# Column tiles of 64 for the attention read and the state product of an mLSTM plus mixture-of-experts kernel

## The chip, the cores and the metric

The kernel runs on one core of a Trainium2 chip. The metric is device time of one launch in microseconds; the median of three runs of the kernel before is 427.37 us (427.31 to 427.56).

## What is computed

A gated recurrent attention (2 batches, 8 heads, 768 steps, head size 40) is followed by four dense experts (320 to 1024 to 320), whose outputs are summed with normalised weights:

```python
for t in range(S):
    m_new = np.maximum(f_gate[:, :, t] + m, i_gate[:, :, t])
    f_stab = np.exp(f_gate[:, :, t] + m - m_new)
    i_stab = np.exp(i_gate[:, :, t] - m_new)
    m = m_new
    C = f_stab[:, :, None, None] * C + i_stab[:, :, None, None] * np.einsum('bhd,bhe->bhde', vt, kt)
    n = f_stab[:, :, None] * n + i_stab[:, :, None] * kt
    h_tilde = np.einsum('bhde,bhe->bhd', C, qt)
    denom = np.maximum(np.abs(np.einsum('bhd,bhd->bh', n, qt)), 1.0)[:, :, None]
    y[:, :, t] = h_tilde / ((1.0 + np.exp(-o_gate[:, :, t])) * denom)
...
for e in range(E):
    out += p[:, e:e + 1] * (np.maximum(x @ w1[e], 0.0) @ w2[e])
```

## The kernel before, in words

The 1536 tokens are 12 chunks `n` of 128; chunks 0 to 5 are the first batch, 6 to 11 the second, and `c = n % 6` is the place in the batch. Within a chunk the recurrence is written as matrix products. In the order in which TensorE (PE) gets them in the loop from chunk 2 on:

- `inter(n)` (L460, tile y1): queries times the state carried into the chunk, two heads to a product; left out at c = 0. ScalarE (ACT) then reads y1 out of PSUM head by head with a scale, eight instructions at L467 (tile yb).
- `intra(n)` (L474, tile y0): the chunk's own keys. One product for each of the 8 heads: the weighted scores `pm` of a head (128 keys x 128 queries) are loaded as weights, and the head's scaled values (64 columns, 41 of them used: 40 values and the sum) are streamed.
- `state(n)` (L427, tile st): what the chunk adds to the state, two heads to a product: 104 columns of keys as weights, 105 columns of values streamed. Of each product only the two diagonal blocks are wanted. Left out at c = 5. VectorE (DVE, L442) adds them to the decayed old state, at c = 0 ACT copies them (L76).
- `scores(n + 1)` (L412, tile s): keys times queries of the next chunk, two heads in two row tiles of 64 rows, side by side.

These are float32 products; each one stands in the trace as two weight loads (LDWEIGHTS, row PEld) and two MATMUL passes. Around them PE runs pieces of expert 0 on finished chunks (`steps`: hidden layer at L147, tile ph; output layer at L178 to L180, tile po) and the transposes of a finished chunk (`turn`, L500, tile px: two blocks of 128 columns and one of 64). `norm(n)` on DVE (L486 to L493) adds yb to y0, divides, and applies the output gate; `decay` (L385), `weigh` (L418) and `turn_lo` (L507, L508) are also on DVE. `values` and `keys` (L396, L401) and most of the splits of the experts' weights into a high and a low part (L92) are on GpSimd (POOL).

The order on every engine is the order of the code: chunks 0 and 1 are written out by hand (L556 to L617), the loop at L624 does chunks 2 to 11, and from about 165 us on only experts 1 to 3 are left. Nothing reorders a queue. The PSUM tiles y1, y0, st and px come in this order from the pool `ps_y`, which has two buffers (tag `y`): st(n) takes the buffer of y1(n), so its first product waits until ACT has read y1; px takes that of y0; y0 of the next chunk that of px. In chunks 0 and 1 some of these tiles come from other pools, by the arguments of the calls.

Of the kernel before, what the change touches and what calls it, by code (L numbers as in the profile page):

```python
# [15 lines left out]
B, H, S, D = 2, 8, 768, 40  # L16
NE, DM, FF = 4, 320, 1024
NT = B * S
L = 128
# [24 lines left out]
def tile_mlstm_moe(ctx, tc, gt, qk, vk, ot, dp, w1, w2, out):  # L44
    ctx.enter_context(tc.manual_schedule())
    nc = tc.nc
# [27 lines left out]
    def copy(eng, dst, src):  # L74
        if eng is nc.scalar:
            eng.activation(dst, src, AF.Copy)  # L76
        else:
            eng.tensor_copy(dst, src)
# [114 lines left out]
    with ExitStack() as actx:  # L193
# [166 lines left out]
        fbs, dds, vvs, pms, ss = {}, {}, {}, {}, {}  # L360
# [59 lines left out]
        def state(n, pool=ps_y, tag="y"):  # L420

            c, vv, kk = n % NC, vvs[n], kp[n % 2]
            if c == NC - 1:
                return
            st = pool.tile([L, NP, L], F32, tag=tag, name="st")
            for p in range(NP):
                nc.tensor.matmul(  # L427
                    st[0:104, p, 0:105],
                    kk[:, 2 * p:2 * p + 2, :].rearrange("k r d -> k (r d)")[:, 0:104],
                    vv[:, 2 * p:2 * p + 2, :].rearrange("k r d -> k (r d)")[:, 0:105],  # L430
                    start=True, stop=True,
                )
            cout = cs[(c + 1) % 2]
            if c == 0:
                for r in range(2):
                    q, q2 = slice(64 * r, 64 + 40 * r), slice(64 * r, 64 + 41 * r)
                    copy(nc.scalar, cout[q, :, q2], st[q, :, q2])
            else:
                cd = cds.pop(n)
                for q in (slice(0, 64), slice(64, 104)):  # L440
                    q2 = slice(q.start, q.start + (64 if q.start == 0 else D + 1))
                    nc.vector.tensor_add(cout[q, :, q2], cd[q, :, q2], st[q, :, q2])  # L442

        def carry(n):
# [26 lines left out]
        def intra(n):  # L471
            y = y0s[n] = ps_y.tile([L, H, 64], F32, tag="y", name="y0")
            for h in range(H):
                nc.tensor.matmul(  # L474
                    y[:, h, :], pms[n][:, h, :], vvs[n][:, h, :], start=True, stop=True
                )

        def norm(n):

# [90 lines left out]
        gate_i(2, NC, nc.gpsimd)  # L570
        decay(1)
        intra(0)
        state(0, ps_w, "w")
        values(1)
        keys(1)
# [11 lines left out]
        quarter_lo(0)  # L587
        gate_b(2, NC)
        intra(1)
        norm(1)  # L590
        turn(0, ps_h, "ph")
# [4 lines left out]
        turn_lo(1)  # L596
        scores(2)
        state(1)
        quarter_hi(1)
        gate_last(2, NC)  # L600
# [23 lines left out]
        for n in range(2, NCH):  # L624
            j, cc = n // 2, n % 2
            k = SLOTS[n - 2]
# [18 lines left out]
            if n == 3:  # L645
                weights_out(4, nc.gpsimd)
            intra(n)
            state(n)
            norm(n)
            if n == 2:  # L650
# [131 lines left out]
```

## Time and profile before

| | |
|---|---|
| median of three runs | 427.37 us |
| profiled execution, first to last instruction (span) | 425.8 us |
| PE busy with matmuls | 420.6 us |
| chunks (attention and expert 0) | up to about 165 us |
| experts 1 to 3 | from about 165 us |

The profile page gives the span of the profiled execution and no other time of it; the median stands 1.5 us above that span, which is what lies around it. Busy time of PE is the union of its passes, whose ends are modelled. A row of the chain of waits gives the time by which a piece of work carries the end further; a row of the timeline gives when a merged group starts and how long it takes from its first start to its last end, and in brackets how long the engine sat idle before it and for whom.

### The profile page before, as it was taken

What the parts mean: (1) busy time and instruction counts of PE and PEld (TensorE: products, weight loads), DVE (VectorE), ACT (ScalarE), POOL (GpSimd) and SP (SyncE); (2) the same over time, 40 slices, a digit from 0 to 9 for tenths busy, and PEclk for the clock granted to TensorE, in tenths of its full rate; (3) what the DMA queues carried; (4) which work ended last, traced back from release to release, by engine and by line L of the source; (5) the groups of instructions that cost most, each with busy time, mean ns of one, the idle gap of its engine ahead of it and who ended that gap; (6) DMA issues with size and microseconds to landing.
All of it is one profiled execution on the core that took longest, in us unless ns stands there. A gap on an engine that the chain in (4) does not pass through costs nothing.

```text
span 425.8 us, 6596 instructions
## 1 busy us (share of the span) xinstructions
PE 420.6 (99%) x2754; PEld 377.8 (89%) x2754; DVE 180.0 (42%) x321; ACT 125.3 (29%) x298; POOL 81.0 (19%) x92
## 2 busy tenths in 40 slices
PE   9999999999999999999999999999999999999996
PEld 5789999999999998897997988979979879789796
DVE  8869777574865321513313224123132242231321
ACT  5656233234313252503403124024031140120210
POOL 6855601220210170200610001007100010000000
PEclk9999999999999999999999999999999999999999
DMA  7984716347200002210110003001200000001001
GB/s 220 315 257 127 212 52 160 113 101 237 84 2 2 0 16 110 77 72 0 66 58 0 2 0 149 0 3 33 92 0 2 0 0 32 31 2 46 18 15 48
DMA packets 15078, 29.31 MB, mean 69 GB/s; under 512 B 1000, under 2 KB 10728, under 8 KB 13736
## 3 DMA queue, kind: packets, MB, share of 16 engines
q1 hardware_dynamic: 15048, 28.88, 21.5%
q8 instruction: 22, 0.36, 0.4%
q14 instruction: 8, 0.07, 0.1%
HBM read 26.86 MB, written 2.02 MB: 68 GB/s over the span
## 4 chain that ended last, share of the span: by engine, by line
PE 98%; DVE 1%; ACT 0%; issue 0%; DVEq 0%
PE ph L147 39%; PE po L178 13%; PE po L179 13%; PE po L180 13%; PE y L474 5%; PE s L412 3%; PE ph L170 3%; PE st L427 2%; PE y L460 2%; PE pwm L69 2%; PE px L500 1%; PE fb L368 1%; PE pit L298 0%; ACT cs L76 0%; PE pit L320 0%
## 5 line engine op out<-in xcount | busy, mean ns | idle before, releaser
L147 PE MATMUL ph<-xst,w1s 128*128 128x512 f32 (+1 forms) x888 | 171.0, 349 | 0.0
L147 PEld LDWEIGHTS ph<-xst,w1s 128*128 128x128 f32 x888 | 140.2, 189 | 27.7 <-issue 6.6
L178 PE MATMUL po<-w2s,h 128*128 128x320 f32 x384 | 119.5, 311 | 0.0
L156 ACT ACTIVATE h<-ph 128x512 fp32r<-128x512 f32 x96 | 57.4, 598 | 209.7 <-PE ph L147 209.0
L180 PE MATMUL po<-w2s,h 128*128 128x320 f32 x384 | 118.6, 309 | 0.0
L179 PE MATMUL po<-w2s,h 128*128 128x320 f32 x384 | 118.6, 309 | 0.0
L157 DVE SCALAR_TENSOR_TENSOR h<-ph,h 128x512 fp32r<-128x512 f32 x96 | 66.2, 690 | 116.0 <-ACT h L156 115.6
L178 PEld LDWEIGHTS po<-w2s,h 128*128 128x128 f32 x384 | 72.1, 188 | 0.9
L179 PEld LDWEIGHTS po<-w2s,h 128*128 128x128 f32 x384 | 72.1, 188 | 0.4
L180 PEld LDWEIGHTS po<-w2s,h 128*128 128x128 f32 x384 | 72.1, 188 | 0.0
L185 DVE SCALAR_TENSOR_TENSOR acc<-po,pw,acc 128x320 f32<-128x320 f32 x36 | 19.8, 550 | 100.0 <-PE po L180 100.0
L92 POOL TENSOR_TENSOR w1s<-raw,w1s 128x512 fp32r<-128x512 f32 (+1 forms) x24 | 23.6, 1020 | 58.2 <-ACT w1s L89 58.2
L385 DVE TENSOR_TENSOR_SCAN dd<-fb,id 128x512 f32<-128x512 f32 x24 | 29.3, 1264 | 0.2
L92 POOL TENSOR_TENSOR w2s<-raw,w2s 128x640 fp32r<-128x640 f32 x6 | 9.4, 1571 | 103.9 <-ACT w2s L89 103.9
L474 PE MATMUL y<-vp,pm 128*128 128x64 f32 x192 | 23.1, 273 | 0.7 <-DVE xst L508 0.7
L474 PEld LDWEIGHTS y<-vp,pm 128*128 128x128 f32 x192 | 22.5, 192 | 1.0 <-issue 0.8
L183 ACT ACTIVATE acc<-po,pw 128x320 f32<-128x320 f32 x12 | 6.3, 528 | 45.2 <-PE po L180 45.2
L467 ACT ACTIVATE yb<-y,ibT 128x41 f32<-128x41 f32 x80 | 16.0, 311 | 3.9 <-PE y L460 3.9
L418 DVE TENSOR_TENSOR pm<-s,dd 128x512 f32<-128x512 f32 x24 | 15.4, 682 | 0.5 <-PE s L412 0.3
L401 POOL TENSOR_TENSOR kp<-vk,dd 128x320 f32<-128x320 f32 x10 | 7.4, 735 | 38.4 <-DVE dd L385 38.4
L412 PE MATMUL s<-qk 64*128 64x128 f32 (+1 forms) x192 | 14.1, 285 | 0.0
L412 PEld LDWEIGHTS s<-qk 64*128 64x128 f32 (+1 forms) x192 | 11.8, 187 | 1.8 <-DVE pm L418 0.8
(94 smaller groups left out, 259.3 us busy)
## 6 DMA issues: line engine op xcount, KB each, us to landing
raw<-in_w SPq DMA_DIRECT2D x3, 1536.0 KB, 6.2
fb<-f_d SPq DMA_DIRECT2D x8, 512.0 KB, 7.6
raw<-in_w SPq DMA_DIRECT2D x3, 1280.0 KB
qk<-in_qk SPq DMA_DIRECT2D x4, 832.0 KB
vk<-in_vk SPq DMA_DIRECT2D x4, 640.0 KB, 8.1
acc<-in_ot SPq DMA_DIRECT2D x6, 320.0 KB, 9.2
out<-acc SPq DMA_DIRECT2D x12, 160.0 KB, 1.8
qk<-in_qk SPq DMA_DIRECT2D x4, 416.0 KB
```

Of the source, the lines that this page charges most:

```text
L92: eng.tensor_sub(lo, raw, hi.bitcast(F32))
L147: nc.tensor.matmul(ph[:, i, :], self.w1s[:, wi, f * L:(f + 1) * L], xst[:, xi, self.t0:self.t0 + n], start=(k == 0 and not self.e), stop=( ...
L156: nc.scalar.activation(hh, ph, AF.Relu)
L157: nc.vector.scalar_tensor_tensor(out=hl, in0=ph, scalar=0.0, in1=hh.bitcast(F32), op0=ALU.max, op1=ALU.subtract)
L178: nc.tensor.matmul(po, hh[:, sl], ws[:, LO, f, :], start=(f == 0), stop=False)
L179: nc.tensor.matmul(po, hh[:, sl], ws[:, HI, f, :], start=False, stop=False)
L180: nc.tensor.matmul(po, hl[:, sl], ws[:, HI, f, :], start=False, stop=(f == NF - 1))
L185: nc.vector.scalar_tensor_tensor(out=acc[:, i, :], in0=po, scalar=pw[:, i, e:e + 1], in1=acc[:, i, :], op0=ALU.mult, op1=ALU.add,)
L385: nc.vector.tensor_tensor_scan(out=dds[n][:, 4 * i:4 * i + 4].rearrange("p h t -> p (h t)"), data0=fbs[n][i].rearrange("p h t -> p (h t)") ...
L412: nc.tensor.matmul(ss[n][r][:, p, :], kg[q, p], qg[q, p], start=True, stop=True)
L467: nc.scalar.activation(yb[:, h], y1[:, h, 0:D + 1], AF.Copy, scale=ibT[:, c, i:i + 1])
L474: nc.tensor.matmul(y[:, h, :], pms[n][:, h, :], vvs[n][:, h, :], start=True, stop=True)
```

## The change

`intra` issues two products for each head instead of one: queries 0 to 63 and queries 64 to 127 as weights of 64 columns each, with results in PSUM partitions 0 to 63 and 64 to 127 of the same bank. The values streamed are the 41 used columns, no longer 64. `state` issues one product for each head instead of one for each pair: 40 columns of keys as weights, 41 columns of values streamed; the even head's result goes to partitions 0 to 39, the odd head's to 64 to 103. In both, two neighbouring products use the two column tiles of TensorE (128 rows x 64 columns). The additions at L442 and the copies at L76 take the two diagonal blocks of 40 x 41 instead of 64 x 64 and 40 x 41. Nothing else is changed.

```diff
             st = pool.tile([L, NP, L], F32, tag=tag, name="st")
+            blocks = [(slice(64 * r, 64 * r + D), slice(64 * r, 64 * r + D + 1)) for r in range(2)]
             for p in range(NP):
-                nc.tensor.matmul(
-                    st[0:104, p, 0:105],
-                    kk[:, 2 * p:2 * p + 2, :].rearrange("k r d -> k (r d)")[:, 0:104],
-                    vv[:, 2 * p:2 * p + 2, :].rearrange("k r d -> k (r d)")[:, 0:105],
-                    start=True, stop=True,
-                )
+                for r, (q, q2) in enumerate(blocks):
+                    h = 2 * p + r
+                    nc.tensor.matmul(
+                        st[q, p, q2], kk[:, h, 0:D], vv[:, h, 0:D + 1], start=True, stop=True
+                    )
...
-                for q in (slice(0, 64), slice(64, 104)):
-                    q2 = slice(q.start, q.start + (64 if q.start == 0 else D + 1))
+                for q, q2 in blocks:
                     nc.vector.tensor_add(cout[q, :, q2], cd[q, :, q2], st[q, :, q2])
...
             for h in range(H):
-                nc.tensor.matmul(
-                    y[:, h, :], pms[n][:, h, :], vvs[n][:, h, :], start=True, stop=True
-                )
+                for t in (slice(0, 64), slice(64, L)):
+                    nc.tensor.matmul(
+                        y[t, h, 0:D + 1], pms[n][:, h, t], vvs[n][:, h, 0:D + 1],
+                        start=True, stop=True,
+                    )
```

On PE, chunk 3 before, with what each instruction waits for (a name like Activation_49 is the semaphore of that engine; rows without brackets follow their predecessor): read of the old state, read of the own keys, state product, next scores, output layer.

```order
L460 MATMUL y_591<-cs_129,qk_131 128x128 x4
L474 MATMUL y_609<-vp_125,pm 128x64 [waits PE_49,DVE_49,Activation_49,Pool_49]
L474 MATMUL y_609<-vp_125,pm 128x64 x7
L427 MATMUL st<-vp_125,kp_127 104x105 [waits PE_49,Activation_49,Pool_49]
L427 MATMUL st<-vp_125,kp_127 104x105 x3
L412 MATMUL s<-qk_130 128x128 [waits DMAHW3_49]
L412 MATMUL s<-qk_130 128x128 x7
L178 MATMUL po<-w2s_93,h 128x320 [waits DVE_49]
```

The same place on PE in the changed kernel:

```order
L458 MATMUL y_627<-cs_129,qk_131 128x128 x4
L473 MATMUL y_645<-vp_125,pm 64x41 [waits PE_49,DVE_49,Activation_49,Pool_49]
L473 MATMUL y_645<-vp_125,pm 64x41 x15
L430 MATMUL st<-vp_125,kp_127 40x41 [waits PE_49,Activation_49,Pool_49]
L430 MATMUL st<-vp_125,kp_127 40x41 x7
L412 MATMUL s<-qk_130 128x128 [waits DMAHW3_49]
L412 MATMUL s<-qk_130 128x128 x7
L178 MATMUL po<-w2s_93,h 128x320 [waits DVE_49]
```

No instruction has moved past another: 8 products have become 16 and 4 have become 8, of smaller shape, and the first state product still waits for the same three engines. On DVE, the state addition of chunk 1 (cs, from the old state cd and st), with its neighbours:

```order
 L508 TENSOR_TENSOR xst<-px,xst 64x128
-L442 TENSOR_TENSOR cs_128<-cd,st 64x4x64
-L442 TENSOR_TENSOR cs_128<-cd,st 40x4x41
+L440 TENSOR_TENSOR cs_128<-cd,st 40x4x41 x2
 L385 SCALAR_TENSOR_TENSOR dd<-fb,id_117 128x512 x2
 L157 SCALAR_TENSOR_TENSOR h<-ph,h 128x512 x2
```

It is two instructions as before, the first of them smaller, in the same place.

## Rows read from the trace of the kernel before

**Rows 1.** The page: busy time of the engines; the chain that ended last, by line.

```profile
PE 420.6 (99%) x2754; PEld 377.8 (89%) x2754; DVE 180.0 (42%) x321; ACT 125.3 (29%) x298; POOL 81.0 (19%) x92
...
PE ph L147 39%; PE po L178 13%; PE po L179 13%; PE po L180 13%; PE y L474 5%; PE s L412 3%; PE ph L170 3%; PE st L427 2%; PE y L460 2%; PE pwm L69 2%; PE px L500 1%; PE fb L368 1%; PE pit L298 0%; ACT cs L76 0%; PE pit L320 0%
```

**Rows 2.** Instructions writing y and st: ns minimum/median/maximum, first and last start.

```profile
L474 PEld LDWEIGHTS y<-vp,pm x192: 186/192/192, 12.9 to 141.4; 128*128 128x128 f32 x192
L474 PE MATMUL y<-vp,pm x192: 217/275/323, 12.9 to 141.5; 128*128 128x64 f32 x192
L460 PE MATMUL y<-cs,qk x80: 272/275/377, 16.5 to 139.7; 104*128 104x128 f32 x80
...
L427 PEld LDWEIGHTS st<-vp,kp x80: 166/172/172, 14.7 to 131.4; 128*104 128x104 f32 x80
L427 PEldq EVENT_SEMAPHORE  x8: 51/1636/1641, 32.0 to 129.1; - x8
```

**Rows 3.** Chain of waits, chunks 4 to 6: start us, us, what.

```profile
63.62 0.33 PE px L500 x3
63.95 1.91 PE ph L147 x16
...
66.75 1.73 PE y L474 x16
68.49 1.09 PE s L412 x16
...
80.80 0.77 PE st L427 x8
...
82.66 4.03 PE ph L147 x32
```

**Rows 4.** Timeline, chunk 7: start us, us, engine, line, instructions, idle before.

```profile
89.65 1.90 PE L474 MATMUL y<-vp,pm 128*128 128x64 f32 x16
...
89.85 1.60 ACT L467 ACTIVATE yb<-y,ibT 128x41 f32<-128x41 f32 x8 [0.30 <-PE y L460]
...
91.55 0.95 PE L427 MATMUL st<-vp,kp 128*104 128x105 f32 x8
```

**Rows 5.** Timeline, chunks 0 and 1: ACT and DVE.

```profile
14.35 0.63 ACT L272 ACTIVATE ib<-ib 16x512 f32<-16x512 f32 x1 [1.11 <-POOL ib L271]
...
15.75 0.70 ACT L76 ACTIVATE cs<-st 64x256 f32<-64x256 f32 x2 [0.77 <-PE st L427]
...
17.01 1.30 DVE L277 TENSOR_TENSOR_SCAN gat<-fs,bs 16x512 f32<-16x512 f32 x1
...
17.69 1.60 ACT L467 ACTIVATE yb<-y,ibT 128x41 f32<-128x41 f32 x8 [1.01 <-PE y L460]
...
19.49 0.51 DVE L486 TENSOR_TENSOR y<-y,yb 128x328 f32<-128x328 f32 x1 [1.18 <-PE y L474]
```

**Rows 6.** Timeline, chunks 2 to 4.

```profile
31.77 2.33 DVE L385 TENSOR_TENSOR_SCAN dd<-fb,id 128x512 f32<-128x512 f32 x2
...
34.56 0.76 DVE L442 TENSOR_TENSOR cs<-cd,st 64x256 f32<-64x256 f32 x2 [0.47 <-PE st L427]
...
36.95 0.49 DVE L493 TENSOR_TENSOR xr<-xr,y 128x320 f32<-128x320 f32 x1
...
37.58 0.52 PE L500 MATMUL px<-ident,xr 128*128 128x128 f32 x3
...
43.24 3.98 POOL L92 TENSOR_TENSOR w2s<-w2r,w2s 128x640 fp32r<-128x640 f32 x2 [4.99 <-ACT w2s L89]
...
47.36 0.33 PE L178 MATMUL po<-w2s,h 128*128 128x320 f32 x1
...
53.46 1.55 ACT L467 ACTIVATE yb<-y,ibT 128x41 f32<-128x41 f32 x8
...
53.84 1.97 PE L474 MATMUL y<-vp,pm 128*128 128x64 f32 x16 [0.67 <-DVE xst L508]
...
55.65 0.93 PE L427 MATMUL st<-vp,kp 128*104 128x105 f32 x8
```

More of the change, by code (lines that the diff above doesn't have):

```diff
@@ L425, in state @@
             st = pool.tile([L, NP, L], F32, tag=tag, name="st")
+            blocks = [(slice(64 * r, 64 * r + D), slice(64 * r, 64 * r + D + 1)) for r in range(2)]
             for p in range(NP):
-                nc.tensor.matmul(
-                    st[0:104, p, 0:105],
-                    kk[:, 2 * p:2 * p + 2, :].rearrange("k r d -> k (r d)")[:, 0:104],
-                    vv[:, 2 * p:2 * p + 2, :].rearrange("k r d -> k (r d)")[:, 0:105],
-                    start=True, stop=True,
-                )
+                for r, (q, q2) in enumerate(blocks):
[3 more added lines that the diff above has]
+                    )
             cout = cs[(c + 1) % 2]
             if c == 0:
-                for r in range(2):
-                    q, q2 = slice(64 * r, 64 + 40 * r), slice(64 * r, 64 + 41 * r)
+                for q, q2 in blocks:
                     copy(nc.scalar, cout[q, :, q2], st[q, :, q2])
@@ L439, in state @@
                 cd = cds.pop(n)
-                for q in (slice(0, 64), slice(64, 104)):
-                    q2 = slice(q.start, q.start + (64 if q.start == 0 else D + 1))
+                for q, q2 in blocks:
                     nc.vector.tensor_add(cout[q, :, q2], cd[q, :, q2], st[q, :, q2])
```

## The prediction, made before the changed kernel ran

> **What bounds the kernel now.** I read the page first: PE is busy 420.6 of 425.8 us, and the chain that ended last is PE nearly throughout [rows 1]. The work that is changed is in that chain: the read of the own keys (L474) with 5% and the state product (L427) with 2%, some 30 us together. So time taken from these passes is time taken from the kernel, unless PE then has to wait for something. Three questions follow: what sets the pace of these passes, what a change of tiles costs, and who is late next in each chunk.
>
> **The pace of a pass.** I went to the durations of the single instructions [rows 2] and the chain around chunks 4 to 6 [rows 3]. A chunk's 16 passes of L474 take 1.73 us, 108 ns each; the 8 of L427 take 0.77 us, 96 ns each. Is it the load or the stream? A load of 128 columns is recorded with 192 ns, one of 104 columns with 172: 20 ns for 24 columns, 0.83 ns a column. A stream of 64 columns that isn't held up is recorded with 217 ns (the minimum of L474), one of 128 columns with 272 (L460): 55 ns for 64 columns, 0.86 ns a column. At L474 128 columns are loaded (107 ns) and 64 streamed (55 ns) while a pass takes 108, and the median MATMUL has 275 ns, 58 above its minimum: it is held up by its load. So the load sets the pace, one pass for each load, and what is streamed hides behind it.
>
> By this, a pass with 64 columns to load takes 108 - 64 x 0.83 = 55 ns, with 41 columns streamed (35 ns) behind it. A pass of the state product with 40 columns to load takes 96 - 64 x 0.83 = 43 ns.
>
> **Two tiles side by side.** The trace has no column tiles in this form, but it has row tiles: the scores (L412) run 16 passes of 128 columns in 1.09 us in two tiles of 64 rows [rows 3]. Taking 0.19 us off for the change of tiles (below), this is 0.90 us for 8 pairs, 112 ns a pair: two tiles together take as long as one pass of one tile. This is the nearest row, and I take the same for column tiles. Then the 32 passes of the new L474 are 16 pairs of 55 ns, 0.88 us, and the 16 of the new state product are 8 pairs of 43 ns, 0.34 us. Taken away: **0.85 us** a chunk from the first, **0.43 us** from the second. The other end is that two column tiles take turns: 32 x 55 = 1.76 and 16 x 43 = 0.69 us, which is +0.03 and -0.08 us: no gain. That end is the first rival.
>
> **Changing tiles.** After the scores, 32 passes of L147 take 4.03 us, though 16 take 1.91 where nothing is changed ahead of them [rows 3]: 4.03 - 2 x 1.92 = 0.19 us for leaving the row tiles, and the same for entering them. The other bound is the transposes: the third block of L500 has 64 columns, and three blocks take 0.33 us, with 16 passes of L147 in 1.91 behind them [rows 3]: nothing. The changed kernel has 15 more such places: into L473 ahead of ten chunks from 2 on, out of it after chunk 11, two around it in chunk 1, and one behind each state product of chunks 0 and 1. I take 0.19 for each, since the scores are the nearer relation (ordinary products in tiles of half size); zero stays in the range.
>
> The Trainium skill, "TensorEngine Tiling (Array Packing)", section "Key Properties", states that a change of the tiling mode drains TensorE. The row of the scores agrees with it, the row of the transposes shows no drain; by the rule each of the 15 places costs as taken here, by the second row none, and the sum below would be 0.95 us larger.
>
> **Who is late next.** The first state product takes the PSUM buffer of y1 and waits for ACT to have read it. In chunk 7 ACT reads from 89.85 for 1.60 us, to 91.45; the state product starts at 91.55 [rows 4], and the wait of PE's sequencer for this is 1.64 us long in the median of 8 [rows 2]. PE loses nothing by it today only because L474 fills just this time. When L474 is shorter, PE sits idle until 91.55 all the same: in chunks 3 and 7 to 10, which look alike, **the whole gain of L474 becomes a wait**, and the drain ahead of it is hidden there too. The scores, the output layer and all behind them wait in the same queue. Only what the state product saves remains.
>
> The sum, chunk by chunk:
>
> - Chunks 0 and 1. State product 0 ends 1.28 us earlier, but ACT is busy until 14.98, so its copy starts at 14.98 instead of 15.75 [rows 5]: 0.77 us. The read of y1 in chunk 1 then ends at 19.29 - 0.77 = 18.52; DVE's scan ends at 18.31; so norm(1), today at 19.49 and waiting for L474 [rows 5], starts at about 18.62. That is 0.87 us, and the transposes that wait for it move with it. State product 1 adds 0.43, less 0.19 for leaving column tiles: **1.11**.
> - Chunk 2. PE could gain 0.5, but the transposes at 37.58 follow DVE's xr (end 37.44), and DVE can add the state no earlier than its scan ends, at 34.10 instead of 34.56 [rows 6]: **0.46**.
> - Chunk 3. The output layer at 47.36 comes just behind POOL's split of w2, which ends at 47.22 [rows 6] and hangs on ACT, which starts it behind the read of y1. This chain isn't shortened: **0**. The 0.43 us of the state product are waited away.
> - Chunk 4. L474 waits for DVE at its start (0.67 us idle, which hides the drain). ACT's read ends at 55.01, so the state product can start at 55.11 instead of 55.65 [rows 6]: 0.54 + 0.43 = **0.97**.
> - Chunk 5 has no state product: 0.85 - 0.19 = **0.66**.
> - Chunk 6 has no y1: 0.85 + 0.43 - 0.19 = **1.09**.
> - Chunks 7 to 10: 4 x 0.43 = **1.72**.
> - Chunk 11: 0.85, less two drains, 0.38: **0.47**.
>
> Together 6.48 us: a span of 419.4 instead of 425.8, and **420.9 us** with the 1.5 us around it as in the runs shown. DVE's first addition gets shorter; that is on no path. The experts behind 165 us are as they were, and everything that feeds them is released by earlier work of PE and moves with it.
>
> The unknown sizes around this: no drains, 0.95 less; state pairs that don't get faster than 96 ns, 7 x 0.43 + 0.46 = 3.5 more; a POOL split that isn't late in chunk 3, 0.4 less. L474 itself matters little: up to some 1.6 us a chunk it is hidden behind ACT wherever there is a y1, so an error in the 55 ns costs in chunks 5, 6 and 11 alone. The forecast's own range is 419.4 to 424.4.
>
> **The rivals.** (1) *The column tiles take turns* at the load. L474 +0.03 x 12, the state product -0.08 x 10, and 15 drains of 0.19: 0.4 - 0.8 + 2.85 = 2.4 us more, **429.8 us**, slower. Here nothing hides the drains, since the work ahead of the state product is no longer short. For it: both tiles read the same 128 rows, unlike the row tiles, whose loads come from different rows; no row here shows two loads into the same rows at once. Against it: the pace of the row tiles. It decides from the point where a pair of state passes takes more than about 60 ns and L474 doesn't get shorter: then 10 x 8 x 36 ns equal the drains. I give it 0.20. (2) *A tile's load even waits for the other tile's stream.* Then a pass takes 55 + 35 = 90 ns: L474 2.88 us a chunk (+1.15 x 12), the state product 16 x 78 = 1.25 (+0.48 x 10), drains 2.85: 21 us more, **449 us**. Against it: loads and streams overlap nearly always today, PEld 89% and PE 99% busy at once, in the same rows [rows 1]. 0.03.
>
> The Trainium skill, "TensorE: Matmul & The Clock Gate", section "Part 3: Packing small matmuls — row/col tiling", has a rule that would make (2): a load overlaps with matmuls in flight only where the row group differs, and column tiles of one another have the same rows. The trace doesn't agree for full-width products, and no run here shows it for column tiles yet.
>
> (3) *The gain is made and given back*: DVE, POOL or a transfer is late in more places than I found, as POOL is in chunk 3. DVE is busy 42% of the span and POOL 19% [rows 1]. If the gains ahead of chunk 4 (1.57) and half of the rest go, 6.48 - 1.57 - 2.46 = 2.4 are left, **425 us**; 423.6 to 427 in all. 0.11.
>
> **How the numbers follow.** Forecast 0.66, rival (1) 0.20, (2) 0.03, (3) 0.11. A measurement of this kernel tells about 0.2%, 0.85 us, from no change. Faster by more than that are the forecast and most of (3): 0.72. Within it, the rest of (3) and a little of (1): 0.05. Slower: 0.23. To leave out no more than 2 in 10, the range must take in rival (1): 419.3 to 430.2.
>
> **What would show it.** Right: L473 as 32 passes in about 0.9 us, the state product in about 0.35, PE idle some 0.5 us ahead of it in chunks 3 and 7 to 10, waiting for L465 (the read of y1, L467 before), and PE waiting for POOL in chunk 3. If the passes of the two tiles follow each other at 55 ns each, rival (1) is it; if L473 takes over 2.5 us a chunk, rival (2). The forecast is wrong too if the first state product doesn't wait for ACT: the gain is then nearer 10 us. If a drain is not there, chunks 5, 6 and 11 show it: 0.85 instead of 0.66 us gained at L473.

## The result, and the profile after

The changed kernel takes **420.61 us** (median of four runs, 420.58 to 423.57) against 427.39 us before: a ratio of 0.984 (95% interval 0.980 to 0.989), 6.8 us less. The span of the profiled execution is 418.8 us, 7.0 less than before. In some runs of several kernels here, the one of 423.57 us among them, TensorE's mean granted clock was 0.98 to 0.996 and the time 1.5 to 5 us longer; where a profiled run is one of them (e1, e2, e4, e6 and e8, with the lower clock somewhere between 14 and 46 us), I compare single chunks and give the range of the runs too.

The page of the changed kernel answers [rows 1]: PE is busy 12.0 us less, but the span is only 7.0 shorter: 5 us have become idle time.

```profile
PE 408.6 (98%) x3026; PEld 364.7 (87%) x3026; DVE 178.9 (43%) x321; ACT 125.0 (30%) x298; POOL 81.0 (19%) x92
...
PE ph L147 40%; PE po L178 13%; PE po L180 13%; PE po L179 13%; PE ph L170 3%; PE s L412 2%; PE y L473 2%; PE y L458 2%; PE st L430 1%; PE px L500 1%; POOL w2s L92 1%; ACT yb L465 1%; POOL w1s L92 0%; ACT L262 0%; ACT L358 0%
```

The lines have moved: the own keys are L473 (L474 before), the state product L430 (L427), its addition L440 (L442), the read of the old state L458 (L460), ACT's copy of it L465 (L467). In the chain that ended last, L473 has 2% instead of 5%, and POOL's split of w2 and ACT's read of y1, which were not among the first fifteen, now have 1% each.

Durations of the single instructions, answering [rows 2] (columns: ns minimum/median/maximum, first and last start):

```profile
L473 PEld LDWEIGHTS y<-vp,pm x384: 132/138/138, 12.9 to 134.3; 128*64 128x64 f32 x192
L473 PE MATMUL y<-vp,pm x384: 223/230/252, 12.9 to 134.4; 128*64 128x41 f32 x192
...
L430 PEld LDWEIGHTS st<-vp,kp x160: 112/118/123, 13.8 to 125.1; 128*40 128x40 f32 x160
L430 PE MATMUL st<-vp,kp x160: 199/202/232, 13.8 to 125.1; 128*40 128x41 f32 x160
L430 PEldq EVENT_SEMAPHORE  x8: 51/1357/1362, 30.8 to 123.4; - x8
```

A load of 64 columns is recorded with 138 ns where 128 took 192: 54 ns for 64 columns, as the prediction's slope has it. A MATMUL of L473 has 230 ns at the median and 223 at least, 7 ns apart where L474 had 58. But it is still held up by its load, though by less: the same 41 columns are recorded with 202 ns at L430, and with 199 at least in the kernel of `e8_narrow_stream` below. The last row is PE's sequencer waiting, 1.36 us at the median where it was 1.64. The chain of waits around chunks 4 to 7, answering [rows 3] (start us, us, what):

```profile
54.70 6.05 PE ph L147 x48
...
63.88 1.06 PE y L473 x32
...
75.52 1.06 PE y L473 x32
76.59 0.31 PE st L430 x16
...
85.14 1.06 PE y L473 x32
86.21 0.68 issue
86.88 0.51 PE st L430 x15
```

1.73 us have become 1.06, and 0.77 have become 0.31. In chunk 7 there is a new row between the two, 0.68 us of "issue". The timeline of chunk 7, answering [rows 4] (start us, us, engine, line, instructions, idle before):

```profile
85.07 1.01 PEld L473 LDWEIGHTS y<-vp,pm 128*64 128x64 f32 x32
85.07 1.13 PE L473 MATMUL y<-vp,pm 128*64 128x41 f32 x32
...
85.18 1.60 ACT L465 ACTIVATE yb<-y,ibT 128x41 f32<-128x41 f32 x8 [0.30 <-PE y L458]
...
86.88 0.51 PE L430 MATMUL st<-vp,kp 128*40 128x41 f32 x16 [0.68 <-issue]
```

The first state product starts 0.10 us after ACT has ended (85.18 + 1.60 = 86.78), as it did before. The view calls the wait "issue" because what waits is PE's sequencer, and its row has no engine for it; the summary of PE's waits shows how often:

```profile
PE st L430 <- issue: 3.4, 5, 0.7
...
PE px L500 <- DVE xr L493: 0.6, 1, 0.6
...
PE st L430 <- POOL w1s L92: 0.5, 1, 0.5
PE po L178 <- POOL w2s L92: 0.2, 1, 0.2
```

Five times 0.68 us: chunks 3 and 7 to 10. The timelines of chunks 0 and 1 [rows 5] and 2 to 4 [rows 6] after the change:

```profile
14.35 0.63 ACT L272 ACTIVATE ib<-ib 16x512 f32<-16x512 f32 x1 [1.18 <-POOL ib L271]
...
14.88 0.60 ACT L76 ACTIVATE cs<-st 40x164 f32<-40x164 f32 x2
...
16.74 1.60 ACT L465 ACTIVATE yb<-y,ibT 128x41 f32<-128x41 f32 x8 [1.01 <-PE y L458]
...
18.37 0.51 DVE L486 TENSOR_TENSOR y<-y,yb 128x328 f32<-128x328 f32 x1
...
30.35 2.33 DVE L385 TENSOR_TENSOR_SCAN dd<-fb,id 128x512 f32<-128x512 f32 x2
...
32.63 0.66 DVE L440 TENSOR_TENSOR cs<-cd,st 40x164 f32<-40x164 f32 x2
...
34.93 0.49 DVE L493 TENSOR_TENSOR xr<-xr,y 128x320 f32<-128x320 f32 x1
...
45.27 0.41 PE L178 MATMUL po<-w2s,h 128*128 128x320 f32 x1 [0.23 <-POOL w2s L92]
```

Set against the rows of before, from the start of an instruction behind a chunk (a pass of L460, now L458, or of L147 or L178) to that of its counterpart, this is where the 7.0 us come from:

| chunk | 0, 1 | 2 | 3 | 4 | 5 | 6 | 7 to 10 | 11 | sum |
|---|---|---|---|---|---|---|---|---|---|
| forecast | 1.11 | 0.46 | 0 | 0.97 | 0.66 | 1.09 | 4 x 0.43 | 0.47 | 6.48 |
| measured | 1.42 | 0.60 | 0 | 0.86 | 0.67 | 1.13 | 1.80 | 0.53 | 7.01 |

### The profile page after: what moved, and what is told of

Same layout as the page of the kernel before. It is cut to its first block, busy times and chain, and to the rows that moved or that the text cites. A ratio compares the mean times of both kernels' runs of the same rounds, so it can differ in the third digit from the quotient of the medians.

```text
span 418.8 us, 7140 instructions
## 1 busy us (share of the span) xinstructions
PE 408.6 (98%) x3026; PEld 364.7 (87%) x3026; DVE 178.9 (43%) x321; ACT 125.0 (30%) x298; POOL 81.0 (19%) x92
## 3 DMA queue, kind: packets, MB, share of 16 engines
HBM read 26.86 MB, written 2.02 MB: 69 GB/s over the span
## 4 chain that ended last, share of the span: by engine, by line
PE 91%; ACT 3%; DVE 2%; POOL 2%; issue 1%; POOLq 0%; ACTq 0%
PE ph L147 40%; PE po L178 13%; PE po L180 13%; PE po L179 13%; PE ph L170 3%; PE s L412 2%; PE y L473 2%; PE y L458 2%; PE st L430 1%; PE px L500 1%; POOL w2s L92 1%; ACT yb L465 1%; POOL w1s L92 0%; ACT L262 0%; ACT L358 0%
## 5 line engine op out<-in xcount | busy, mean ns | idle before, releaser
L147 PE MATMUL ph<-xst,w1s 128*128 128x512 f32 (+1 forms) x888 | 171.1, 349 | 0.0
L147 PEld LDWEIGHTS ph<-xst,w1s 128*128 128x128 f32 x888 | 140.2, 189 | 27.8 <-issue 6.6
L178 PE MATMUL po<-w2s,h 128*128 128x320 f32 x384 | 119.6, 311 | 0.2 <-POOL w2s L92 0.2
L157 DVE SCALAR_TENSOR_TENSOR h<-ph,h 128x512 fp32r<-128x512 f32 x96 | 66.2, 690 | 116.2 <-ACT h L156 115.8
L178 PEld LDWEIGHTS po<-w2s,h 128*128 128x128 f32 x384 | 72.1, 188 | 1.4 <-POOL w2s L92 0.5
L385 DVE TENSOR_TENSOR_SCAN dd<-fb,id 128x512 f32<-128x512 f32 x24 | 29.4, 1264 | 0.2
L465 ACT ACTIVATE yb<-y,ibT 128x41 f32<-128x41 f32 x80 | 16.0, 311 | 3.9 <-PE y L458 3.9
L473 PE MATMUL y<-vp,pm 128*64 128x41 f32 x384 | 13.8, 231 | 0.7 <-DVE xst L508 0.7
L473 PEld LDWEIGHTS y<-vp,pm 128*64 128x64 f32 x384 | 12.3, 138 | 2.2 <-issue 0.8
L89 ACT ACTIVATE w2s<-raw 128x640 fp32r<-128x640 f32 x12 | 8.8, 732 | 15.9 <-DMA raw<-in_w 15.9
```

The source lines that it names most:

```text
L147: nc.tensor.matmul(ph[:, i, :], self.w1s[:, wi, f * L:(f + 1) * L], xst[:, xi, self.t0:self.t0 + n], start=(k == 0 and not self.e), stop=( ...
L157: nc.vector.scalar_tensor_tensor(out=hl, in0=ph, scalar=0.0, in1=hh.bitcast(F32), op0=ALU.max, op1=ALU.subtract)
L178: nc.tensor.matmul(po, hh[:, sl], ws[:, LO, f, :], start=(f == 0), stop=False)
L385: nc.vector.tensor_tensor_scan(out=dds[n][:, 4 * i:4 * i + 4].rearrange("p h t -> p (h t)"), data0=fbs[n][i].rearrange("p h t -> p (h t)") ...
L465: nc.scalar.activation(yb[:, h], y1[:, h, 0:D + 1], AF.Copy, scale=ibT[:, c, i:i + 1])
L473: nc.tensor.matmul(y[t, h, 0:D + 1], pms[n][:, h, t], vvs[n][:, h, 0:D + 1], start=True, stop=True,)
```

## The experiments

Each kernel was timed beside runs of the kernel before on the same chip (medians 427.36, 427.34 and 427.33 us).

### Do the two tiles really run at the same time?

`e7_one_half_after_the_other` is the changed kernel with the two loops of `intra` exchanged: all heads for queries 0 to 63, then all heads for 64 to 127. Same instructions, same tiles, other order.

```diff
-            for h in range(H):
-                for t in (slice(0, 64), slice(64, L)):
+            for t in (slice(0, 64), slice(64, L)):
+                for h in range(H):
```

> The changed kernel with the own-keys read issued tile by tile: the lower queries of all eight heads, then the upper queries of all eight, so that neighbouring products are in the same column tile. Theory: two tiles overlap only where their products are neighbours in the queue; then 32 passes of 56 ns take turns, 1.96 us a chunk instead of 1.06; 0.9 us more in chunks 5, 6 and 11, 0.55 in chunk 4, some 0.6 in chunks 0 and 1, hidden behind ACT elsewhere: 424.6 us. Rival (PE pulls the other tile's passes ahead from eight products away): 420.6 us.

Measured: 423.39 us (423.33 to 423.57), ratio 0.987 (0.981 to 0.994), between the two figures and nearer to the theory's; 32 passes take 1.78 us in its chain of waits where the theory had 1.96. Chunk 7 in its timeline:

```profile
86.97 1.73 PEld L473 LDWEIGHTS y<-vp,pm 128*64 128x64 f32 x32
86.97 1.85 PE L473 MATMUL y<-vp,pm 128*64 128x41 f32 x32
...
88.78 0.51 PE L430 MATMUL st<-vp,kp 128*40 128x41 f32 x16
```

The same 32 loads take 1.73 us instead of 1.01. This is the pace of the rival "the tiles take turns" (32 x 55 ns = 1.76 us), brought about by the order of the code: loads of one tile follow each other every 58 ns. In the changed kernel's records the two instructions of a pair start 7 ns apart, and pairs come every 58 ns; (1.01 - 0.138)/15 = 58 ns by the row, too. So two loads into the same 128 rows do run at once, if they stand next to each other in the queue. In the records of e7's chunk 7 the second tile's first pass starts (at 87.70) when the first tile has three passes left to start, not sixteen. So "nothing reorders a queue", in the section on the kernel before, isn't quite so on PE: here a pass comes ahead of three earlier ones of the other tile. The view shows no wait ahead of the state product in chunk 7: L473 fills ACT's time again.

`e8_narrow_stream` is the kernel before with only the streamed columns cut from 64 to 41.

```diff
-                    y[:, h, :], pms[n][:, h, :], vvs[n][:, h, :], start=True, stop=True
+                    y[:, h, 0:D + 1], pms[n][:, h, :], vvs[n][:, h, 0:D + 1], start=True, stop=True
```

> The kernel before, but the own-keys read streams the 41 used columns instead of 64, still with weights of 128 columns. Theory (the load sets the pace of a pass): no change, 427.2 to 427.6 us, passes still 112 ns apart. Rival (part of the gain is the shorter stream): 23 columns of 0.86 ns in 16 passes are 0.3 us a chunk, seen in chunks 4, 5, 6 and 11 at least: 426 us or less.

Measured: 428.02 us (427.17 to 432.58), ratio 1.002 (0.998 to 1.007): no gain. The chain is read at chunk 5, where the granted clock is 1.00 (it is 0.79 from 12 to 20 us in this run), and beside it stands the row of its MATMULs:

```profile
67.62 1.71 PE y L474 x16
```

```profile
L474 PE MATMUL y<-vp,pm x192: 199/283/416, 12.6 to 142.3; 128*128 128x41 f32 x192
```

1.71 us against 1.73 [rows 3], with 36% of the stream gone. With 128 columns to load, the load alone sets the pace: the shorter stream brings nothing by itself. No run streams 64 columns behind the loads of 64.

### Each half of the change alone

`e3_state_only` leaves `intra` as before. `e4_own_keys_only` leaves the state product as before; the smaller addition and copies of the change stay in both. From the changed kernel, e3 takes back this (cut at the end):

```diff
-                for t in (slice(0, 64), slice(64, L)):
-                    nc.tensor.matmul(
-                        y[t, h, 0:D + 1], pms[n][:, h, t], vvs[n][:, h, 0:D + 1],
+                nc.tensor.matmul(
+                    y[:, h, :], pms[n][:, h, :], vvs[n][:, h, :], start=True, stop=True
```

and e4 this (cut at the end):

```diff
-                for r, (q, q2) in enumerate(blocks):
-                    h = 2 * p + r
-                    nc.tensor.matmul(
-                        st[q, p, q2], kk[:, h, 0:D], vv[:, h, 0:D + 1], start=True, stop=True
+                nc.tensor.matmul(
+                    st[0:104, p, 0:105],
```

> Only the state product in column tiles; the own-keys read as before. Theory: 0.43 us a chunk less, and a change of tiles of 0.19 ahead of it that nothing hides now: 0.24 in chunks 2, 4, 6 and 7 to 10, nothing in chunk 3, about 0.55 in chunks 0 and 1: 2.2 us, 425.2 us. If changes of tiles cost nothing: 423.8 us. If the gain of the whole change came from the own-keys read: 427.4 us.

> Only the own-keys read in column tiles; the state product as before. Theory: the wait for ACT eats it in chunks 3 and 7 to 10; what is left is about 1.1 us in chunks 0 and 1, 0.1 in chunk 2, 0.54 in chunk 4, 0.67 in chunk 5, 0.5 in chunk 6 (two changes of tiles), 0.53 in chunk 11: 3.4 us, 424.0 us. If no wait ate it: 0.67 x 12, 419.5 us.

Measured: e3 423.88 us (423.68 to 425.26), ratio 0.990 (0.987 to 0.994); e4 424.33 us (424.01 to 425.65), ratio 0.993 (0.991 to 0.995). The gains of the two, 3.5 and 3.0 us, add up to 6.5 of the 6.8 (the smaller copies and addition are in both). From the chain of waits of e3, chunks 6 and 7:

```profile
77.31 1.73 PE y L472 x16
79.04 0.43 PE st L430 x16
...
87.71 1.73 PE y L472 x16
89.44 0.50 PE st L430 x12
```

and of e4, the same chunks:

```profile
78.15 1.06 PE y L474 x32
79.21 0.91 PE st L428 x8
...
88.36 1.06 PE y L474 x32
89.42 0.67 issue
90.09 0.95 PE st L428 x8
```

Three things follow. The state product is 0.31 us behind column tiles (changed kernel) and 0.43 behind full-width passes, so entering costs 0.12 there; by the starts of the passes it is 0.09 at L473 too. The full-width product is 0.91 behind column tiles and 0.77 behind its like, so leaving costs 0.14. And e3 alone gained 0.44 to 0.47 in each of chunks 7 to 10: there the drain cost nothing, because the product before had already begun from a standstill (0.95 against 0.77 us [rows 3, 4]). Four times 0.2 us more than expected is the larger part of why e3 came in at the figure without drains (423.8) and not at the one with them (425.2). In e4 chunks 7 to 10 gained nothing at all: it is 1.45 us ahead of before at the start of chunk 7, and 1.48 at the start of chunk 11. The gain of L473 is a wait in these chunks, 0.67 us each, as forecast. No run puts the state product's two tiles one after the other, as e7 does for L473; that its pairs run at once is read from their pace (0.31 us for 16 passes, 0.69 if they took turns at the prediction's 43 ns).

### Taking the new wait away

The state product waits because its tile takes the PSUM buffer of y1. `e1_y1_own_buffer` gives y1 a buffer of the output layer's pool instead, and `e2_before_y1_own_buffer` does the same to the kernel before:

```diff
-            inter(n)
+            inter(n, ps_o, "po")
```

> The changed kernel with y1 of the loop's chunks in the buffers of the output layer (pool ps_o) instead of ps_y, so that the state product no longer waits for ACT's read of y1. Theory (the gain of the own-keys read is eaten by this wait): the idle 0.68 us ahead of the state product in chunks 7 to 10 goes, and the 0.20 us that a state product takes longer when it starts from standstill (0.51 against 0.31 in chunk 6): 4 x 0.88, some 0.3 in chunk 4, nothing in chunk 2 (DVE's scan) and chunk 3 (POOL's split): 3.8 us less than the changed kernel, 416.8 us. Rival (PE would wait for DVE or something else there anyway): 419.5 to 420.6 us.

> The kernel before with the same move of y1 to ps_o. Theory: with the old own-keys read the wait ends just when that read ends, so nothing is to be had: 427.2 to 427.5 us. Rival (the buffer was a cost of its own before the change already): 2 us or more less, below 425.5 us.

Both missed: e1 423.32 us (421.66 to 424.2), ratio 0.988 (0.983 to 0.994); e2 433.76 us (432.72 to 434.04), ratio 1.013 (1.006 to 1.019). The wait of e1 that neither side of its expectation has, and the busy time of its engines and the granted clock (after POOL) by stretch:

```profile
PE y L458 <- DVE dd L385: 2.4, 1, 2.4
```

```profile
core 0: us, PE busy (x) PEld busy (x) DVE busy (x) ACT busy (x) POOL busy (x), PEclk, DMA share, GB/s
20.00:30.00 10.00, 9.50 (x81) 8.65 (x82) 5.48 (x10) 5.49 (x14) 4.63 (x7) 0.83 0.87 289
30.00:33.00 3.00, 0.66 (x6) 0.51 (x5) 2.99 (x5) 0.89 (x3) 2.79 (x3) 0.76 1.02 220
33.00:42.00 9.00, 8.92 (x84) 8.39 (x85) 4.94 (x12) 2.52 (x11) 4.46 (x6) 0.51 0.37 124
42.00:52.00 10.00, 9.14 (x115) 8.58 (x114) 8.38 (x14) 5.78 (x17) 3.83 (x2) 1.00 0.48 113
```

In chunk 2 both buffers of that pool hold the spread gates of chunk 3 (fb) until DVE's scan (L385) has read them. So y1 waits 2.4 us for DVE. TensorE's granted clock, 0.83 in the ten us ahead, is 0.51 for the nine us behind it: the lower level of 1.2 GHz nearly throughout. When the read of the old state in chunk 3 starts (at 44.78), e1 is 7.0 us behind the changed kernel; 1.5 of them were there ahead of the wait. In e2 the clock is 1.00 from 20 to 30 us, and the same wait of 2.4 us is followed by 12.3 us at 0.50:

```profile
32.70:45.00 12.30, 12.28 (x64) 11.87 (x65) 4.98 (x11) 2.52 (x11) 4.44 (x6) 0.50 0.29 89
```

From there on the theory holds: in chunk 7 of e1 the state product starts without a wait,

```profile
92.02 1.13 PE L473 MATMUL y<-vp,pm 128*64 128x41 f32 x32
92.97 0.48 PE L430 MATMUL st<-vp,kp 128*40 128x41 f32 x16
```

and chunks 7 to 10 gain 0.87 us each over the changed kernel, 3.5 in all; in e2 they gain 0.19 each. So the wait was worth 0.19 before the change and is worth 0.87 now.

`e5_y1_from_chunk_3` keeps the old buffer in chunk 2 alone:

```diff
-            inter(n)
+            inter(n, *((ps_y, "y") if n == 2 else (ps_o, "po")))
```

> The changed kernel with y1 in the buffers of the output layer from chunk 3 on only. In chunk 2 those buffers still hold the gates' spread for chunk 3, and y1 waited there for DVE's scan in the two runs before. Theory (the own-keys read's gain is eaten by the wait for ACT): chunks 7 to 10 give 0.87 us each, as they did between those runs' chunks, chunks 3 and 4 nothing (POOL's split and a hidden step that waits for DVE): 3.5 us less than the changed kernel, 417.1 us. Rival (something else holds PE): 420 us or more.

Measured: 417.11 us (417.09 to 417.27), ratio 0.973 (0.966 to 0.979), as expected, and 6.2 us less than e1, from which it differs in the buffer of chunk 2 alone. Its granted clock from 30 to 42 us is 1.00. Chunks 7 to 10 gain 0.87 each again. In chunks 3 and 4 the gain has become other waits:

```profile
PE po L178 <- POOL w2s L92: 1.1, 1, 1.1
PE ph L147 <- DVE h L157: 0.9, 1, 0.9
```

The first is the split of w2 on POOL, which the prediction named for chunk 3. `e6_y1_and_w2_earlier` calls it ahead of the chunk's scan, and with it ACT's part of it ahead of the read of y1:

```diff
+            if n == 3:
+                weights_out(4, nc.gpsimd)
             if nxt:
                 decay(n + 1)
             steps(k[0])
...
-            if n == 3:
-                weights_out(4, nc.gpsimd)
```

> As e5_y1_from_chunk_3, and the second half of expert 0's w2 is split ahead of the read of the old state in chunk 3, not behind it. Theory (in chunk 3 the output layer waits for POOL, whose work starts behind ACT's read of y1): up to 1.3 us more, 415.8 us; if DVE or the hidden step of chunk 4 is late next, 416.5 to 417.1 us. If POOL's wait isn't what eats chunk 3: 417.1 us.

Missed: 419.2 us (417.42 to 420.43), ratio 0.977 (0.970 to 0.984). Only the run of 417.42 has a mean clock of 1.0; in the profiled one it is 0.83 from 20 to 30 us, and 1.00 in chunk 3. The wait for POOL is gone there, and PE waits for DVE in its place:

```profile
PE po L180 <- DVE h L157: 1.4, 1, 1.4
```

DVE's piece of the hidden layer (L157) that the output layer needs stands behind the scan of chunk 4 in DVE's queue. So chunk 3 is 0.3 us longer than in e5 (1.4 us of waiting for 1.1), and the one run of e6 at full clock is 0.3 us slower than e5. `e9_low_half_ahead_of_scan` is e6 with that piece of the expert ahead of the scan, in chunk 3 alone:

```diff
             if n == 3:
                 weights_out(4, nc.gpsimd)
+                steps(k[0])
             if nxt:
                 decay(n + 1)
-            steps(k[0])
+            if n != 3:
+                steps(k[0])
```

> As e6_y1_and_w2_earlier, and in chunk 3 DVE makes the low half of the last hidden block (L157) ahead of the scan of chunk 4, not behind it. In e6 PE no longer waited for POOL in chunk 3 but 1.39 us for this L157. Theory (chunk 3 has two late engines, one behind the other): with both moved, that wait goes and nothing takes its place: 1.1 us less than e5_y1_from_chunk_3, 416.0 us. Rival (a third is late, such as the hidden step in chunk 4 that waits for DVE): 416.5 to 417.1 us.

Measured: **415.80 us** (415.76 to 415.89), ratio 0.973 (0.971 to 0.975), as expected; 1.3 us below e5, all of it there by the end of chunk 3 (1.28 us), and 4.8 us below the changed kernel: the fastest here. Of the waits of PE that e5 had in chunks 3 and 4, one is left:

```profile
PE ph L147 <- DVE h L157: 0.9, 1, 0.9
```

## Why the prediction was right, and where its steps were off

**Right in sign and size, by its own steps.** Forecast 420.9, measured 420.6. The load sets the pace (e8), two column tiles run as one (7 ns apart, e7 for the other case), the gain of L473 becomes a wait for ACT in chunks 3 and 7 to 10 (0.68 us five times, e4), and it lasts where no y1 is read or no state product follows: chunks 5 and 6, 0.67 and 1.13 us against 0.66 and 1.09. Chunk 3 gains nothing because of POOL, as read. That the two totals lie only 0.3 us apart is in part luck: the sum of the chunks was 0.53 us too small, and the term around the span, further down, 0.3 us too small the other way.

**Pairs and drains.** Two errors cancelled in L473: pairs take 58 ns, not 55 (16 pairs: 0.05 us more), and a change into or out of column tiles costs 0.09 to 0.14 us, not the 0.19 of the scores' row tiles. The sum 0.88 + 0.19 = 1.07 met the 1.06 of the chain. In chunk 11 the drains show: 0.53 gained, 0.47 forecast with two of 0.19. State pairs take 0.31/8 = 39 ns instead of 43. The Trainium skill, "TensorEngine Tiling (Array Packing)", section "Key Properties", has a drain at each change of mode and tiles that work independently of each other; both are seen here, the drain at half to three quarters of the price taken and hidden wherever PE starts from a standstill.

**Chunks 0 and 1: 1.42 instead of 1.11.** ACT's copy of state 0 starts at 14.88, not 14.98: it overlaps the end of the instruction ahead of it. The copy has become 0.10 us shorter (0.60 against 0.70); its first half has 40 rows of 41 columns instead of 64 of 64, and I had not counted that. Norm(1) starts at 18.37 instead of 18.62, right behind ACT. State product 1 then brings 0.30, for which I had 0.24. Beside this, the profiled execution of before had begun chunk 0 at 12.94 us, and the same code in e2 at 12.62: some 0.3 us of the 7.0 in span lie in that execution. (In the changed kernel a later start of chunk 0 costs nothing: 12.88 in its profiled execution and 12.63 in e5, with the read of the old state in chunk 1 at 15.54 and 15.53.) This also mends the term around the span: I set the median, 427.37, against the span of an execution that had probably taken the longest of the three times, 427.56. Then 1.76 us lie around it, as 1.7 to 1.9 do in every run on record that has both figures, where I had 1.5. In the medians the whole gain is 6.8 us.

**Chunk 2: 0.60 instead of 0.46.** Here a step failed. I wrote that DVE's shorter first addition is on no path. It is: DVE adds the state (32.63, before 34.56), then goes on to the norm and to xr (34.93, before 36.95 [rows 6]), on which the transposes wait. The addition starts 1.93 us earlier, 0.51 more than the chunk itself (forecast 0.46), and all behind it 2.02: the 0.10 by which it got shorter (0.76 to 0.66) is a gain of PE. The 0.5 us that PE now stands for POOL's split of w1 ahead of the state product, which the forecast did not have, costs nothing: the product ends at 32.52, and DVE is busy with its scan till 32.68.

**Chunk 4: 0.86 instead of 0.97.** Up to the scores the chunk gains 0.96, as forecast. Then PE arrives earlier at the hidden layer, and its 48 passes take 6.05 us; before they took 5.95, without a wait. The 0.10 is the first sign of a DVE that is late there:

```profile
57.84 0.68 DVE L157 SCALAR_TENSOR_TENSOR h<-ph,h 128x512 fp32r<-128x512 f32 x1
```

The 33rd of the 48 passes starts at 58.57, right behind the end of this row, and the next one 0.22 us later, where 0.12 is the pace; before, L157 had ended 0.19 us ahead of that pass. When e5 brings PE 0.7 us earlier still, the wait for L157 is 0.9 us. No run took DVE's queue apart in that chunk.

**The rivals.** (1) is refuted for this order of the code, and real for another: e7 gives it 32 passes in 1.78 us. It didn't get to 429.8 us there, since e7's state products still run in pairs; e7 is 2.8 us slower than the changed kernel. (2) is refuted: an L473 pass starts while the other tile's load and stream run. The rule in the Trainium skill, "TensorE: Matmul & The Clock Gate", section "Part 3: Packing small matmuls — row/col tiling", that a load overlaps with matmuls in flight only in another row group, doesn't hold for the column tiles of this trace: 32 loads of 138 ns, 4.4 us together, take 1.01 us beside 32 MATMULs. (3) was true in small: beyond POOL in chunk 3, which the forecast had, POOL's split of w1 is late in chunk 2 at no cost, and DVE takes 0.1 us in chunk 4.

## What to carry to other kernels

Where PE is held up by weight loads, and these can be had in pieces of 64 columns or less, column tiles are worth a trial: here they took a chunk's products from 1.73 to 1.06 us and from 0.77 to 0.31, but L473's only with the two tiles' products next to each other in the code. Before pricing such a gain, look at who holds the PSUM buffer that the next product takes: a read that was hidden behind the slow stage is the next bound, and here it took L473's gain in five chunks, of which four had it back when the buffer came from another pool (e5). A buffer taken from another pool must be looked at in every chunk: a single wait of 2.4 us in chunk 2, with the lower clock behind it, cost more than all that it was to bring.

## What the runs showed of the hardware

- The two column tiles load at once into the same rows, 58 ns for a pair of 64 columns and 39 ns for a pair of 40, where the products alternate; with eight products of one tile ahead of the other's (e7, 64 columns), they run one after the other but for about three passes.
- Entering or leaving column tiles costs 0.09 to 0.14 us, and nothing if PE stands still there anyway; a state product that starts from a standstill takes 0.18 to 0.20 us more than one in a stream (0.95 against 0.77 us before, 0.51 against 0.31 after).
- PE standing for 2.4 us at about 31 us was followed by 9 to 12 us at the lower clock of 1.2 GHz in both kernels that had this wait (0.51 and 0.50 granted, PE busy throughout), while without it (e5) the clock was 1.00 there, the higher level of 2.4. The smaller dips ahead of 30 us (0.83 from 20 to 30 us in e1, e4 and e6, 0.79 from 12 to 20 in e8) come without such a wait, and what brings them is open.
